# Keys and queries loaded as 32x32 blocks and transposed by VectorE in a fused linear-attention and MLP kernel

## The chip, the cores and the metric

The kernel runs on one core of one Trainium2 chip. The metric is device time in microseconds (us) from launch to end of one execution.

## What is computed

The reference is a complex-decay linear attention followed by a two-layer MLP, all in float32:

```
for t in range(S):                       # S = 768, state S_re/S_im is 48 x 48 per (batch, head)
    S_re, S_im = a_t * (S_re + i S_im)   # a_t complex, its magnitude cut at 0.999
    S_re += outer(k_t, v_t)
    y_t = q_t @ S_re
x = y reshaped to (B*S, H*D)             # 3072 x 384
h = x @ w_in;  g = gelu(h);  out = g @ w_out   # 384 -> 2048 -> 384
```

There are 4 batches and 8 heads, so 32 (batch, head) lanes, of head size 48.

## The kernel before

**Lanes.** The recurrence over `t` is turned into scaled keys and queries. The 768 steps are cut into four groups (`GROUPS`) of two chunks each: groups 0 and 1 with chunks of 64 steps, groups 2 and 3 with chunks of 128. Partitions hold (batch, head, chunk) twice, once for rows ahead of the middle of a chunk and once for rows behind it. Each group is worked through in slices of 8 rows (`tick`): `normalise` cuts the magnitude of `a`, `scan` multiplies the decays up row by row on VectorE (tiles `tt`, `bt`), and `towards` and `against` scale the keys and queries in tile `xt`. `against` then writes `xt` to a scratch buffer in DRAM, `kq{g}`, with three DMAs for each slice: one of 768-byte rows and two of 384-byte rows. `kq{g}` is laid out as (batch, head, chunk), step, (key, query), 96 numbers.

**Units.** A unit is 128 steps of one batch, all 8 heads; there are 24 (units 0 to 7 come from groups 0 and 1, units 8 to 15 from group 2, units 16 to 23 from group 3). `unit(u)` loads its keys and queries in one DMA into `kqn` (two such tiles take turns; 1024 rows of 768 bytes, a step to a partition) and its values into `vn`. The keys are used twice. With a step to a partition they are the weights with which `add_state` adds to the state `st`. For the scores they are needed with the 96 numbers on the partitions, so `turn` transposes keys and queries, 8 heads each, with 16 TensorE transposes against `ident_r` into the PSUM banks `att`, and copies these out to `kps` and `qTs` tiles on ScalarE or VectorE. `scores` multiplies, VectorE masks (`kp<-att,causal`), `y` collects the output in PSUM, and the unit ends with its rows split into a high and a low part in `xT` (ScalarE `hi`, VectorE `lo`).

**Blocks.** Two or three units make a block (`BLOCKS` = 2, 3, 3, 3, 3, 3, 3, 2, 2: units 8, 9, 10 are block 3, units 14, 15, 16 block 5). `block(j)` runs 16 steps: `first` (matmuls `ph<-xT,wi_hi` and `wi_lo`, gelu on ScalarE into `gh` and `gf`, the difference `gl` on VectorE) and `second` (matmuls `po<-wo_hi` and `wo_lo`). The first matmul of a block needs the `xT` of all of its units. The units of the next block are put between the steps of a block. At its end a block copies each `po` bank to an output tile and stores it. These output tiles (`ots`) are six halves of the three `raw` tiles, into which the weights were loaded at the start.

**Weights and checks.** At the start the weights are loaded into `raw` and split in two parts by VectorE, ScalarE and TensorE (`weights`, scratch tile `wh`). Later they are read a second time for a range check (`check_range`, DMAs `a<-in_moe_w_in_dram`).

**The order of the work.** All instructions are first collected as steps; `Plan.order` then simulates the engines with a table of costs (`FIXED`, `EACH`, `BYTES`, ...) and writes one fixed order for each engine. It takes the best of several passes, the first of which is ranked with the offsets `MORE`; `BIAS` steers steps that may go to either of two engines. All DMAs go through SyncE's queue (SP) in that order, and an instruction that waits holds up what stands behind it on its engine.

Of the kernel before, what the change touches and what calls it, by code (L numbers as in the profile page):

```python
# [10 lines left out]
F32 = mybir.dt.float32  # L11
# [9 lines left out]
B, H, S, D = 4, 8, 768, 48  # L21
D2 = 2 * D
BH = B * H
C = 128
# [4 lines left out]
GROUPS = ((0, 64), (128, 64), (256, 128), (512, 128))  # L29
NG = len(GROUPS)  # L30
NP = 2 * NG

UNITS = [[(b, t, C)] for t in range(0, S, C) for b in range(B)]
DM = H * D
# [23 lines left out]
def dap(t, offset, dims):  # L58
    return bass.AP(t.tensor, t.offset + offset, dims)


def vap(t, dims):
    t = t[:] if not isinstance(t, bass.AP) else t
    return bass.AP(t.tensor, t.offset, [list(t.ap[0])] + dims)
# [11 lines left out]
TABLE = 1.3  # L76
ISSUE = 0.9
FETCH = 2.2
BYTES = 3.6e5

ROUND, PASS = 0.462e-3, 0.4219e-3

# [9 lines left out]
EARLIER, N_RAW, N_KP = 1, 3, 2  # L92
PASSES = 4
N_A = 4
WL = 0.307

MORE = dict(lanes0=473.93, lanes1=-159.43, lanes2=-833.73, lanes3=415.48, weights0=-32.30, weights1=-241.94, units0=543.37, units1=1360.34, units2=638.43, blocks0=-158.78, blocks1=286.22, blocks2=576.59, checks=842.20)
BIAS = dict(vector=0.35, scalar=-0.41, gpsimd=6.75)


class Step:
# [8 lines left out]
class Plan:  # L110
# [54 lines left out]
    def add(self, calls):  # L165
        step = Step()
        n = len(self.steps)
        engine = calls[0][0]
        cost = 0.08 * (engine == "scalar" and len(calls) > 1)
        for call in calls:  # L170
            outs, ins = self.operands(call)
            cost += self.cost(call, outs, ins)
            if engine == "tensor":
                step.form = ("turn" if call[1] == "transpose" else "round" if call[3]["rhs"].dtype == F32R else
                             "slim" if call[3]["lhsT"].shape[1] <= 32 else "narrow" if call[3]["lhsT"].shape[1] <= 64 else "full")
            if engine == "sync":
                step.data = max(0.05, math.prod(c for _, c in outs[0].ap) * 4 / BYTES)
            for x in tuple(call[2]) + tuple(call[3].values()):
                step.table = TABLES.get(x, step.table) if isinstance(x, AF) else step.table
            for x, writes in [(x, False) for x in ins] + [(x, True) for x in outs]:  # L180
                self.hold(step, n, x, writes)
        step.options[engine] = calls, cost
        self.ports(step, engine, calls)
        if self.behind is not None:
            step.before.add(self.behind)
        step.before.discard(n)
        step.chain, step.weight = self.chain.get(engine, (None, 1.0))
        step.kind, step.part = self.kind, self.part
        self.steps.append(step)
# [71 lines left out]
    def natural(self):  # L261
# [4 lines left out]
        for i in range(len(steps) - 1, -1, -1):  # L266
# [9 lines left out]
            rest[i] = t  # L276
        return [t + MORE[s.kind] for t, s in zip(rest, steps)]

    def forward(self, rank):
# [14 lines left out]
        while len(order) < len(steps):  # L294
            best = None
            for e, waiting in pool.items():
# [8 lines left out]
                if len(steps[i].options) > 1:  # L305
                    ends = {o: max(free[o], ready[i], port[other[o]] if o in steps[i].port else 0.0) + c + BIAS[o] for o, (_, c) in steps[i].options.items()}
                    if ends[e] > min(ends.values()) + 1e-9:
# [106 lines left out]
def lanes_and_chunks(ctx, tc, flags, a_lanes, x_lanes, v_units, w_in, w_out, out):  # L414
    nc = tc.nc
    pool = lambda name, bufs, **kw: ctx.enter_context(tc.tile_pool(name=name, bufs=bufs, **kw))
    cst = pool("cst", 1)
    dram = pool("dram", 1, space=DRAM)
    ps = pool("ps", 1, space=PSUM)
    P = Plan(nc, loose=[flags])  # L420

    def ring(name, shape, n, dtype=F32, pool=cst):
        return itertools.cycle([pool.tile(shape, dtype, name=f"{name}{i}", tag=f"{name}{i}")[:] for i in range(n)])
# [41 lines left out]
    kq = [dram.tile([64, c, 2, D2], F32, name=f"kq{g}") for g, (_, c) in enumerate(GROUPS)]  # L465


    wide = w_in.dtype == U32
    own = [ps.tile([128, 512], F32, name=f"att{i}", tag=f"att{i}")[:] for i in range(3)]
    ph = [ps.tile([128, 512], F32, name=f"ph{i}", tag=f"ph{i}")[:] for i in range(2)]  # L470
# [1 line left out]
    for p in own:  # L472
        nc.vector.memset(p, 0.0)
    ps_h = itertools.cycle(ph)
    raws = ring("raw", [128, DM * (2 if wide else 1)], N_RAW, w_in.dtype)

    wh = cst.tile([128, DM], U32, name="wh")[:]

# [59 lines left out]
    def rows(s):  # L538
        g, i, r0, nt = slices[s]
        return g, i, r0, nt, nt + last_of(s)  # L540
# [4 lines left out]
    def load_a(s):  # L545
        g, i, r0, nt, nr = rows(s)
        a3 = next(a3s)
        at = 2 * D * (GROUPS[g][0] // 4 + g + r0)
        P.sync.dma_start(out=a3[:, 1:3, 0:nr, :], in_=a_lanes[:, at:at + 2 * D * nr].rearrange("p (c r d) -> p c r d", c=2, d=D))
        tiles[s] = {"a3": a3}  # L550

    def load_x(s):
        g, i, r0, nt, nr = rows(s)

        xs[s] = next(xts)[:, 0:nt]
        at = 2 * D * (GROUPS[g][0] // 4 + r0)
        P.sync.dma_start(out=xs[s][:, :, 1], in_=x_lanes[:, at:at + 2 * D * nt].rearrange("p (r c d) -> p r c d", c=2, d=D))
# [74 lines left out]
    def against(s):  # L632

        g, i, r0, nt, nr = rows(s)
        T = tiles[s]
        td, te, xt = T["td"], T["te"], xs[s]
        P.both("tensor_tensor", out=td, in0=T["b2"], in1=te, op=ALU.mult)
        P.vector.scalar_tensor_tensor(out=td, in0=td, scalar=2.0, in1=te, op0=ALU.subtract, op1=ALU.mult, reverse0=True)
        P.both("tensor_tensor", out=td, in0=td, in1=xt[:, :, 1, 1], op=ALU.mult)
        P.both("tensor_tensor", out=xt[:, :, 1], in0=vap(td, [[D, nt], [0, 2], [1, D]]), in1=T["bo"], op=ALU.mult)  # L640
        w, size = 2 * D2, GROUPS[g][1]
        P.sync.dma_start(out=dap(kq[g], (size // 2 - 1 - r0) * w, [[size * w, 64], [-w, nt], [1, w]]), in_=xt[0:64])
        for c in range(2):
            P.sync.dma_start(out=dap(kq[g], (size // 2 + r0) * w + c * D2, [[size * w, 64], [w, nt], [1, D2]]), in_=xt[64:128, :, 1 - c])
        if s + 2 < end:
            load_x(s + 2)
        if s + N_A < end:
            load_a(s + N_A)
# [39 lines left out]
    def tick(s):  # L688
# [20 lines left out]
        with P.work(part=f"b{s}"):  # L709
            if back is not None:  # L710
                towards(back)
                against(back)
        with P.work(part=f"s{s}"):
            scan(s)
        if last_of(s):
            with P.work(part=f"e{s}"):
                squares_b(s)
                ending(s)
                logs(s, None)
                towards(s)  # L720
                against(s)
# [48 lines left out]
    def unit(u):  # L770
# [3 lines left out]
        chunks, row = [], 0  # L774
        for b, t, n in UNITS[u]:
            for i in range(NP):
                g, m = divmod(i, 2)
                t0, size = GROUPS[g][0] + m * GROUPS[g][1] - t, GROUPS[g][1]
# [14 lines left out]
        kqn = next(kqns)  # L793
        kn, qn = kqn[:, :, 0], kqn[:, :, 1]
        vn = next(vns)
        w = 2 * D2
        _, g, m, _, size, b = chunks[0]
        P.sync.dma_start(out=kqn, in_=dap(kq[g], (b * H * 2 + m) * size * w, [[w, C], [2 * size * w, H], [1, w]]))
        P.sync.dma_start(out=vn, in_=v_units[u])

        held = []
# [54 lines left out]
        qT, kT = [], []  # L856

        def turn(src, dst, ring, halves=(0, 1)):
            some = [next(ps_att) for _ in halves]
            with P.together():  # L860
                for hh, p in zip(halves, some):
                    for j in range(4):
                        P.tensor.transpose(out=p[0:D2, j * 128:(j + 1) * 128].bitcast(F32R), in_=src[:, hh * 4 + j, :].bitcast(F32R), identity=ident_r[:])
            for p in some:
                t = next(ring)
                p = p[0:D2, :].rearrange("p (j l) -> p j l", j=4)
                P.either(("scalar", "copy", (t[0:D2], p), {}), ("vector", "tensor_copy", (t[0:D2], p), {}))
                dst.append(t)
# [39 lines left out]
        if early:  # L908
# [11 lines left out]
            for c in with_state:  # L920
                add_state(c, turned[c])
        else:
            turn(kn, kT, kps)
            turn(qn, qT, qTs)
            scores()
# [16 lines left out]
        j = next(j for j in range(len(BLOCKS)) if u < first_unit[j + 1])  # L942
        if u == first_unit[j]:
            xblk[j] = next(xTs)
        xt = xblk[j][:, u - first_unit[j]]
# [9 lines left out]
    ghs, gls = ring("gh", [128, BLK * C], EARLIER + 1, F32R), ring("gl", [128, BLK * C], EARLIER + 1, F32R)  # L955
    gfs = ring("gf", [128, BLK * C], 1)

    ots = itertools.cycle([r.bitcast(F32)[:, c:c + DM] for r in [next(raws) for _ in range(N_RAW)] for c in range(0, r.shape[1], DM)])

    def block(j, between):  # L960
        nt = BLOCKS[j]
# [45 lines left out]
    def ticks(g):  # L1007
        P.chain["vector"] = "lanes", WL
        with P.work(f"lanes{g}"):
            for s in range(end):  # L1010
                if slices[s][0] == g:
                    tick(s)
        P.chain.pop("vector")
# [8 lines left out]
    for u in range(BLOCKS[0]):  # L1022
        with P.work("units0", f"u{u}"):
            unit(u)
    for j, more in enumerate(BLOCKS[1:] + (0,)):
        at = {(2 * i + 1) * NFT // (2 * more): first_unit[j + 1] + i for i in range(more)}
# [154 lines left out]
def tile_complex_linear_attention_moe(ctx, tc, q, k, v, a_re, a_im, w_in, w_out, a_lanes, x_lanes, v_units, w_pieces, out):  # L1181
# [9 lines left out]
    with ExitStack() as fast:  # L1191
        fast.enter_context(tc.manual_schedule())
        lanes_and_chunks(fast, tc, flags, a_lanes, x_lanes, v_units, w_in, w_out, out)
# [81 lines left out]
```

## Time and profile before

| | us |
|---|---|
| median of 3 runs | 673.92 (672.75 to 674.58) |
| the profiled execution, its own time | 674.9 |
| span of the profiled execution | 673.1 |

The span runs from the first to the last instruction on record; the time of the execution is 1.8 us more. PE is TensorE's matmuls, PEld its weight loads, DVE is VectorE, ACT ScalarE, POOL GpSimd, SPq the queue of SyncE that issues DMAs. PEclk is the granted TensorE clock as a share of full speed. All instructions of the plan have line 403, that of the helper that issues them, so that groups are told apart by their tiles.

### The profile page before, as it was taken

To read this page: it belongs to the slowest core of one execution; us is meant where nothing else is said; L and a number is where in the kernel's file an instruction comes from. 1 tells how busy PE (TensorE), PEld (TensorE's weight loads), DVE (VectorE), ACT (ScalarE), POOL (GpSimd) and SP (SyncE) were. 2 spreads that over 40 slices of the span, in tenths; PEclk is the share of its full clock that TensorE was granted. 3 is DMA by queue.
4 is the path that set the end of the run, shared out by engine and by line. 5 is a ranking of instruction groups with operands and counts; after the bars stand their busy time and mean duration, and the time that the engine had idled before them with its cause. 6 is when DMAs were issued, how large, how long until landed. Compare 5 with 4: busy or idle time off the path is not lost.

```text
span 673.1 us, 16301 instructions
## 1 busy us (share of the span) xinstructions
PE 627.9 (93%) x6570; PEld 574.2 (85%) x6570; DVE 451.3 (67%) x1128; ACT 445.2 (66%) x1012; POOL 21.2 (3%) x65
## 2 busy tenths in 40 slices
PE   4566599998999999999999999999999999999995
PEld 2233378887889999999999999999999999999995
DVE  7999979998999999999999972442331221131221
ACT  7556658887888898978889775437634653556532
POOL 2001000030000000102000000000000000000000
PEclk9777789999999999999999999999999999999999
DMA  8388958586366657766777556442444161032000
GB/s 268 94 211 220 252 150 234 161 226 213 102 156 171 142 125 175 186 163 167 189 222 208 109 131 198 134 106 103 131 119 133 40 201 48 24 118 83 25 1 27
DMA packets 134354, 97.07 MB, mean 144 GB/s; under 512 B 69248, under 2 KB 126592, under 8 KB 134272
## 3 DMA queue, kind: packets, MB, share of 16 engines
q1 hardware_dynamic: 134272, 95.96, 52.5%
q8 instruction: 53, 0.87, 0.5%
q14 instruction: 29, 0.24, 0.1%
HBM read 69.40 MB, written 23.59 MB: 138 GB/s over the span
## 4 chain that ended last, share of the span: by engine, by line
PE 81%; DVE 9%; DMA 5%; ACT 2%; issue 1%; SPq 1%; DVEq 0%
PE po L403 32%; PE ph L403 30%; PE att L403 19%; DVE a L403 2%; DMA raw<-in_moe_w_in_dram 2%; DVE tt L403 1%; DMA kqn<-kq 1%; DVE xt L403 1%; DVE bt L403 1%; DMA raw<-in_moe_w_out_dram 1%; DVE wh L403 1%; SPq L403 1%; DMA kq<-xt 1%; DVE raw L403 1%; DVE tab L403 1%
## 5 line engine op out<-in xcount | busy, mean ns | idle before, releaser
L403 PE MATMUL ph<-xT,wi_hi 128*128 128x384 f32 (+1 forms) x864 | 207.3, 321 | 0.0
L403 DVE TENSOR_TENSOR gl<-gf,gh 128x384 fp32r<-128x384 f32 (+1 forms) x144 | 73.9, 513 | 150.6 <-ACT gf L403 145.2
L403 PEld LDWEIGHTS ph<-xT,wi_hi 128*128 128x128 f32 x864 | 153.8, 188 | 2.3 <-issue 0.4
L403 ACT ACTIVATE gh<-ph 128x384 fp32r<-128x384 f32 (+1 forms) x144 | 65.6, 456 | 126.6 <-PE ph L403 125.9
L403 PE MATMUL ph<-xT,wi_lo 128*128 128x384 f32 (+1 forms) x432 | 137.1, 317 | 0.0
L403 PE MATMUL po<-wo_hi,gh 128*128 128x384 f32 x384 | 132.9, 346 | 0.1
L403 PE MATMUL po<-wo_lo,gh 128*128 128x384 f32 x384 | 128.7, 335 | 0.0
L403 PE MATMUL po<-wo_hi,gl 128*128 128x384 f32 x384 | 92.5, 342 | 0.6 <-DVE gl L403 0.6
L403 PEld LDWEIGHTS ph<-xT,wi_lo 128*128 128x128 f32 x432 | 81.2, 188 | 0.0
L403 PEld LDWEIGHTS po<-wo_hi,gh 128*128 128x128 f32 x384 | 72.2, 188 | 2.5 <-ACT gh L403 0.9
L403 PEld LDWEIGHTS po<-wo_lo,gh 128*128 128x128 f32 x384 | 72.3, 188 | 0.1
L403 ACT ACTIVATE gf<-ph 128x384 f32<-128x384 f32 (+1 forms) x144 | 65.1, 452 | 4.9 <-DVE gl L403 3.4
L403 DVE TENSOR_TENSOR tt<-bt,a 128x192 f32<-128x192 f32 x192 | 67.0, 349 | 0.2
L403 PEld LDWEIGHTS po<-wo_hi,gl 128*128 128x128 f32 x384 | 65.1, 188 | 2.0 <-DVE gl L403 1.1
L403 DVE TENSOR_TENSOR bt<-tt 128x96 f32<-128x96 f32 x192 | 47.9, 249 | 0.2
L403 PEld LDWEIGHTS att<-qT,kp 96*64 96x64 f32 (+1 forms) x512 | 39.8, 170 | 2.3 <-issue 1.3
L403 PE MATMUL att<-qT,kp 96*64 96x64 f32 (+1 forms) x512 | 41.7, 256 | 0.0
L403 ACT ACTIVATE a<-a 128x384 f32<-128x384 f32 (+1 forms) x72 | 38.6, 539 | 3.9 <-DMA a<-in_moe_w_in_dram 2.4
L403 DVE TENSOR_TENSOR kp<-att,causal 128x512 f32<-128x512 f32 x48 | 31.8, 683 | 12.9 <-PE att L403 11.1
L403 PE MATMUL po<-raw,ident_r 128*128 128x384 f32 x64 | 31.3, 573 | 8.5 <-issue 2.6
L403 PEld LDWEIGHTS att<-ident_r,kqn 128*96 128x96 f32 x384 | 32.8, 127 | 5.6 <-ACT kp L403 1.3
L403 PE MATMUL att<-ident_r,kqn 128*96 128x128 f32 x384 | 35.7, 236 | 1.9 <-ACT kp L403 1.1
(153 smaller groups left out, 929.7 us busy)
## 6 DMA issues: line engine op xcount, KB each, us to landing
kqn<-kq SPq DMA_DIRECT2D x24, 768.0 KB, 6.3
xt<-in_x_lanes_dram SPq DMA_DIRECT2D x24, 384.0 KB, 4.0
kq<-xt SPq DMA_DIRECT2D x24, 384.0 KB, 4.1
kq<-xt SPq DMA_DIRECT2D x48, 192.0 KB, 4.5
a<-in_a_lanes_dram SPq DMA_DIRECT2D x20, 384.0 KB, 3.4
raw<-in_moe_w_in_dram SPq DMA_DIRECT2D x16, 384.0 KB, 5.2
raw<-in_moe_w_out_dram SPq DMA_DIRECT2D x16, 384.0 KB, 5.0
vn<-in_v_units_dram SPq DMA_DIRECT2D x24, 256.0 KB, 5.6
```

The lines of the kernel that those rows point to most:

```text
L403: getattr(getattr(self.nc, engine), name)(*args, **kw)
```

## The change

- For units 8 to 23 (`u >= UDT`) the one load into `kqn` is replaced by six loads into a tile `blk`, for keys and queries and for each third of the 96 numbers. Each load fills 32 partitions with 1024 runs of 128 bytes: 32 steps on the partitions, and for each head and each 32 steps a run of 32 numbers, so that `blk` holds 32x32 blocks in their places but each not yet transposed. There is one `blk`, and it lies in the memory of the three `raw` tiles.
- `turn` for these units is two VectorE transposes (each 96 partitions x 4 heads x 128, block by block) straight into the `kps` or `qTs` tile: four for a unit. The 16 TensorE transposes and the four copies from PSUM are gone.
- The keys with a step to a partition are still loaded for units 8 to 19, whose state is still added to: 1024 rows of 384 bytes.
- The scratch of groups 2 and 3 (`apart`) has the chunk as its outermost dimension, so that a head and its 32-step blocks lie at one stride. Each slice of these groups is written in six DMAs of 32 lanes rather than three of 64.
- The output tiles are two tiles of their own, `wh` and a new `ot`, in place of six halves of `raw`.
- The planner's cost of a DMA counts packets (`PACKET`, `BYTES`), and its offsets `MORE` and `BIAS` have other values, so that the order of all engines may differ.

```diff
-BYTES = 3.6e5
+PACKET, BYTES = 0.5e-3, 2.96e-6
...
+UDT = 8
-MORE = dict(lanes0=473.93, lanes1=-159.43, lanes2=-833.73, lanes3=415.48, ...
-BIAS = dict(vector=0.35, scalar=-0.41, gpsimd=6.75)
+MORE = dict(lanes0=575.74, lanes1=-377.35, lanes2=-812.79, lanes3=221.09, ...
+BIAS = dict(vector=0.07, scalar=-0.61, gpsimd=7.10)
...
-                step.data = max(0.05, math.prod(c for _, c in outs[0].ap) * 4 / BYTES)
+                some = math.prod(c for _, c in outs[0].ap)
+                step.data = max(0.05, some / min(run(x) for x in outs + ins) * PACKET + some * 4 * BYTES)
...
+    apart = [GROUPS[g][1] == C and any(u >= UDT and ... ) for g in range(NG)]
...
-    raws = ring("raw", [128, DM * (2 if wide else 1)], N_RAW, w_in.dtype)
+    raw_all = cst.tile([128, N_RAW, max(DM * (2 if wide else 1), -(-16 * C // N_RAW))], w_in.dtype, name="raw_all")[:]
+    raws = itertools.cycle([raw_all[:, i, 0:DM * (2 if wide else 1)] for i in range(N_RAW)])
...
-        P.sync.dma_start(out=dap(kq[g], (size // 2 - 1 - r0) * w, [[size * w, 64], [-w, nt], [1, w]]), in_=xt[0:64])
-        for c in range(2):
-            P.sync.dma_start(out=dap(kq[g], (size // 2 + r0) * w + c * D2, [[size * w, 64], [w, nt], [1, D2]]), in_=xt[64:128, :, 1 - c])
+        n = 2 if apart[g] else 1
+        for m in range(n):
+            at = m * BH * size * w
+            P.sync.dma_start(out=dap(kq[g], at + (size // 2 - 1 - r0) * w, [[size * w, 64 // n], [-w, nt], [1, w]]), in_=xt[m:64:n])
+            for c in range(2):
+                P.sync.dma_start(out=dap(kq[g], at + (size // 2 + r0) * w + c * D2, [[size * w, 64 // n], [w, nt], [1, D2]]), in_=xt[64 + m:128:n, :, 1 - c])
...
-        P.sync.dma_start(out=kqn, in_=dap(kq[g], (b * H * 2 + m) * size * w, [[w, C], [2 * size * w, H], [1, w]]))
+        if u < UDT:
+            P.sync.dma_start(out=kqn, in_=dap(kq[g], base, [[w, C], [lane, H], [1, w]]))
+        else:
+            for c in range(2):
+                for j in range(D2 // 32):
+                    P.sync.dma_start(out=blk[j * 32:(j + 1) * 32, c].rearrange("p h (i d) -> p (h i) d", d=32),
+                                     in_=dap(kq[g], base + c * D2 + j * 32, [[w, 32], [32 * w, H * C // 32], [1, 32]]))
+            if chunks[-1][0] < NP - 1:
+                P.sync.dma_start(out=kn, in_=dap(kq[g], base, [[w, C], [lane, H], [1, D2]]))
...
         def turn(src, dst, ring, halves=(0, 1)):
+            if u >= UDT:
+                c = 0 if src is kn else 1
+                for hh in halves:
+                    t = next(ring)
+                    P.vector.transpose(out=t[0:D2], in_=blk[0:D2, c, hh * 4:hh * 4 + 4])
+                    dst.append(t)
+                return
...
-    ots = itertools.cycle([r.bitcast(F32)[:, c:c + DM] for r in [next(raws) for _ in range(N_RAW)] for c in range(0, r.shape[1], DM)])
+    ots = itertools.cycle([wh.bitcast(F32), cst.tile([128, DM], F32, name="ot")[:]])
+    blk = raw_all.rearrange("p i n -> p (i n)").bitcast(F32)[:, 0:16 * C].rearrange("p (c h l) -> p c h l", c=2, h=H)
```

## Rows read from the trace of the kernel before

**Rows 1.** The page: busy time by engine, and its 40 slices.
```profile
PE 627.9 (93%) x6570; PEld 574.2 (85%) x6570; DVE 451.3 (67%) x1128; ACT 445.2 (66%) x1012; POOL 21.2 (3%) x65
...
PE   4566599998999999999999999999999999999995
```

**Rows 2.** The page: the chain that ended last, by engine.
```profile
PE 81%; DVE 9%; DMA 5%; ACT 2%; issue 1%; SPq 1%; DVEq 0%
```

**Rows 3.** Windows by stage: length, busy us (x instructions), PEclk, DMA share, GB/s.
```profile
core 0: us, PE busy (x) PEld busy (x) DVE busy (x) ACT busy (x) POOL busy (x), PEclk, DMA share, GB/s
0.00:160.00 160.00, 122.68 (x1195) 86.83 (x1196) 145.25 (x385) 109.99 (x232) 12.81 (x43) 0.87 0.74 208
...
278.00:327.00 49.00, 48.65 (x622) 47.17 (x621) 48.13 (x123) 39.15 (x90) 4.72 (x9) 1.00 0.70 173
278.00:400.00 122.00, 121.65 (x1484) 118.39 (x1483) 117.78 (x299) 101.42 (x214) 4.72 (x9) 1.00 0.67 171
400.00:535.00 135.00, 135.00 (x1401) 132.38 (x1400) 43.67 (x81) 67.77 (x184) 2.50 (x10) 1.00 0.43 121
```

**Rows 4.** Timeline of PE around unit 8's key transposes: start, us, instruction.
```profile
286.55 0.69 PE L403 MATMUL att<-ident_r,kqn 128*96 128x128 f32 x8
287.08 0.58 PE L403 MATMUL ph<-xT,wi_hi 128*128 128x384 f32 x2
...
288.02 0.51 PE L403 MATMUL ph<-xT,wi_hi 128*128 128x384 f32 x2
```

**Rows 5.** Groups on PE from 278 to 600 us: busy, mean ns, idle.
```profile
L403 PE MATMUL att<-ident_r,kqn 128*96 128x128 f32 x256 | 22.5, 230 | 0.3 <-DVE kp L403 0.3
```

**Rows 6.** Copies from PSUM from 280 us: ns min/median/max, first and last start.
```profile
L403 ACT COPY kp<-att x28: 563/584/617, 299.4 to 585.8; 96x512 f32<-96x512 f32 x28
L403 ACT COPY qT<-att x32: 563/586/645, 289.6 to 593.2; 96x512 f32<-96x512 f32 x32
L403 DVE COPY kp<-att x4: 675/680/682, 287.5 to 325.8; 96x512 f32<-96x512 f32 x4
```

**Rows 7.** Timeline of SP, the stretch in which group 2 ends.
```profile
275.13 2.93 SPq L403 DMA_DIRECT2D kq<-xt  x3
280.86 1.00 SPq L403 DMA_DIRECT2D kqn<-kq  x2
```

**Rows 8.** Windows that hold one load of xt, two of m, one write of kq.
```profile
373.00:375.00 2.00, 2.00 (x18) 2.00 (x17) 2.00 (x8) 1.97 (x4) 0.00 (x0) 1.00 0.82 200
437.50:441.50 4.00, 4.00 (x33) 3.95 (x32) 1.77 (x5) 3.59 (x9) 0.00 (x0) 1.00 0.23 37
229.50:231.50 2.00, 2.00 (x37) 1.93 (x34) 2.00 (x7) 1.76 (x4) 0.00 (x0) 1.00 0.94 173
```

**Rows 9.** DMA issues: count, KB each, median us from issue to landing.
```profile
kqn<-kq SPq DMA_DIRECT2D x24, 768.0 KB, 6.3
out_dram<-raw SPq DMA_DIRECT2D x24, 192.0 KB, 2.1
```

**Rows 10.** Timelines: unit 10's last transposes (PE), its xT (DVE), block 3's first matmul (PE).
```profile
314.22 0.69 PE L403 MATMUL att<-ident_r,kqn 128*96 128x128 f32 x8
...
323.21 0.54 DVE L403 TENSOR_TENSOR xT<-att,xT 128x384 fp32r<-128x384 f32 x1
...
326.82 0.41 PE L403 MATMUL ph<-xT,wi_hi 128*128 128x384 f32 x1
```

**Rows 11.** Timelines at the end of block 4: copies, stores, then the next block's matmuls.
```profile
468.95 0.89 ACT L403 COPY raw<-po 128x384 f32<-128x384 f32 x2
469.21 1.31 SPq L403 DMA_DIRECT2D out_dram<-raw  x3
...
472.75 0.42 PE L403 MATMUL po<-wo_hi,gh 128*128 128x384 f32 x1
```

**Rows 12.** Timeline of SP, the stretch in which group 3 ends.
```profile
398.95 2.92 SPq L403 DMA_DIRECT2D kq<-xt  x3
...
405.81 2.82 SPq L403 DMA_DIRECT2D kqn<-kq  x2
```

More of the change, by code (lines that the diff above doesn't have):

```diff
@@ L95, with run @@
 WL = 0.307
-MORE = dict(lanes0=473.93, lanes1=-159.43, lanes2=-833.73, lanes3=415.48, weights0=-32.30, weights1=-241.94, units0=543.37, units1=1360.34, units2=638.43, blocks0=-158.78, blocks1=286.22, blocks2=576.59, checks=842.20)
-BIAS = dict(vector=0.35, scalar=-0.41, gpsimd=6.75)
+UDT = 8
+MORE = dict(lanes0=575.74, lanes1=-377.35, lanes2=-812.79, lanes3=221.09, weights0=-149.78, weights1=-103.19, units0=636.83, units1=1302.69, units2=549.34, blocks0=-201.58, blocks1=340.05, blocks2=534.64, checks=865.08)
+BIAS = dict(vector=0.07, scalar=-0.61, gpsimd=7.10)
+def run(x):
+    n = 1
+    for step, count in reversed(x.ap):
+        if step != n:
+            break
+        n *= count
+    return n
 class Step:
@@ L465, in lanes_and_chunks @@
     kq = [dram.tile([64, c, 2, D2], F32, name=f"kq{g}") for g, (_, c) in enumerate(GROUPS)]
+    apart = [GROUPS[g][1] == C and any(u >= UDT and GROUPS[g][0] <= t < GROUPS[g][0] + 2 * C for u, some in enumerate(UNITS) for _, t, _ in some) for g in range(NG)]
     wide = w_in.dtype == U32
@@ L797, in unit @@
         _, g, m, _, size, b = chunks[0]
-        P.sync.dma_start(out=kqn, in_=dap(kq[g], (b * H * 2 + m) * size * w, [[w, C], [2 * size * w, H], [1, w]]))
+        base, lane = ((m * BH + b * H) * size * w, size * w) if apart[g] else (b * H * 2 * size * w, 2 * size * w)
+        if u < UDT:
[7 more added lines that the diff above has]
+                P.sync.dma_start(out=kn, in_=dap(kq[g], base, [[w, C], [lane, H], [1, D2]]))
         P.sync.dma_start(out=vn, in_=v_units[u])
```

## The prediction, made before the change was timed

> **What bounds the kernel now.** I read the page first: TensorE's matmuls are busy for 627.9 us of 673.1, and the row of slices shows where the rest is, nearly all in the first quarter; after that it is 9s to the end [rows 1]. The chain that ended last says the same from the other side: 81% of it are TensorE's own instructions, one after the other [rows 2]. Then the windows by stage, for what lies beside TensorE: from 278 to 400 us, while group 3's lanes run, TensorE is busy 121.65 us of 122 and VectorE 117.78 of 122; from 400 to 535 us VectorE has only 43.67 us of work in 135 [rows 3]. So from 278 us on a microsecond taken off TensorE is a microsecond of the span, as long as what TensorE is to work on arrives in time. What must arrive is told by unit 10: it is the last of block 3, and block 3's first matmul comes at 326.82, just 3 us after the unit's `xT` is done at 323.75 (323.21 + 0.54) [rows 10]. The change alters how units 8, 9 and 10 get there, so this is the place to watch. Before it, units 0 to 7 and all of groups 0 and 1 keep their work.
>
> **What is taken off TensorE.** Unit 8's eight key transposes start at 286.55 and the next matmul at 287.08: 0.53 us, and the pair behind them takes 0.58 where a pair in the run of the same work takes 0.51 [rows 4]. That is 0.60 us for eight, 1.20 us for the 16 of a unit, and 19.2 us for 16 units. (The busy time of the 256, 22.5 us [rows 5], counts overlapping instructions, so it is an upper bound; 256 at 0.53 for eight, 17.0 us, is the lower.) TensorE's clock is full in all these stretches (1.00, that is 2.4 GHz [rows 3]), so no other price applies.
>
> **What VectorE and ScalarE get.** ScalarE loses 60 copies of 0.58 us [rows 6], off the path. VectorE gets four transposes of 96x512 for a unit; no such instruction is in the trace. The nearest row is VectorE's copy of the same shape, 0.68 us [rows 6]. As a lower bound I take half of that, as an upper one twice: 0.34 to 1.36. I take 0.68, being one element per lane and step as in the copy: 2.7 us for a unit. The Trainium skill (VectorE: DVE Perf Modes, The three transpose paths) gives 311 ns for a 128x128 transpose in a two-byte type; four times the elements would make an estimate of 1.24 us by that page, near my upper bound, and no run here shows it. Units 8 to 15 fall into VectorE's full stretch: 8 x 2.7 less the four copies that VectorE made itself (2.7) is 19 us more for group 3's lanes, which end with the writes at 398.95 to 401.9 [rows 12]. I cost that at nothing: the first unit that needs group 3 is unit 16, a unit of block 5, and block 4 ends only at about 469 [rows 11]. With 19 us more, unit 16's load is issued at 425 rather than 405.8 [rows 12] and the unit is ready by about 450, before 469 less the gain. Without that cover each microsecond past it would cost one.
>
> **What the loads cost.** Six loads of 1024 runs of 128 bytes are 6144 packets for a unit, against 1024 of 768 bytes; the keys' own load (1024 of 384 bytes) comes on top up to unit 19. Three windows price packets. One load of `xt`, 1024 packets of 384 bytes, is a DMA share of 0.82 over 2 us: 0.82 x 2 x 16 / 1024 = 25.6 ns each. Two swaps of `m`, 768 packets of 192 bytes, are 0.23 over 4 us: 19.2 ns [rows 8]. So half the bytes cost three quarters: the line through both gives 17.1 ns at 128 bytes, 6.6 us for a unit over 16 engines. Upper bound: a 128-byte packet costs no more than one of 384, 9.8 us; lower: in proportion to its bytes (8.5 ns), 3.3 us. The third window, 64 partitions written to `kq` at 173 GB/s [rows 8], says that few partitions may be slow; at that rate the 786 KB would take 4.5 us, inside the bounds.
>
> The two `m` rows also weigh a rule. The Trainium skill (DMA: Bandwidth & Descriptors, Why small descriptors are slow) counts 32-byte beats and three more cycles for a packet: at the DMA's 850 MHz an estimate of 10.6 ns for 192 bytes and 8.2 ns for 128. The window shows 19.2 ns for 192, nearly twice, so the row decides; by the page a unit's load would be 3.2 us, no link would be late, and the time would be that of the second case below.
>
> **The link to block 3.** `blk` is one tile, where `kqn` are two: a unit's loads wait until the unit before has transposed. Before, both loads could go out at 280.86 and unit 8's transposes began at 286.55 [rows 4, 7]. Now unit 8's six go out at 281 (its chunk's writes are issued ahead of the other chunk's, so the three added writes cost nothing; if the load waits for all six, 2 us). First issue 0.4, packets 6.6, landing as for a small store 2.1 [rows 9]: 9.1 us (5.8 to 12.3). Four transposes at 2.7: 11.8 us for a unit (7.2 to 17.7 with both upper prices), so unit 10 is transposed at 281 + 35 = 316 (303 to 334). From its last TensorE transposes, done at 314.75 (314.22 + 0.53), to `xT` at 323.75 the trace takes 9 us [rows 10]: `xT` at 325 (312 to 343). TensorE without three units' transposes would come to block 3 at 326.8 - 3.6 = 323. The stall is 2 us with the queue empty. It isn't: DMA's share from 278 to 327 is already 0.70 of 49 us, 34 us [rows 3], and 20 us of 128-byte packets come in. One microsecond of queueing for each unit makes it 5 us; I take 5 (0 to 20). Later links have room: blocks 3 and 4 run from 326.82 to about 469 [rows 10, 11], some 71 us each for three units, over 20 us a unit, and after 400 us the DMA share is 0.43 [rows 3].
>
> **Smaller parts.** Two output tiles: the third copy of a block waits for the first store, issued at 469.21, to land 2.1 us later [rows 9, 11], and then copies for 0.45: ready at 471.8. The next block first writes the third bank at 472.75 [rows 11], so it lies hidden by 1 us; at other block ends it may miss, and I take 1 us in all (0 to 6). Added kq writes: 48 issues of some 1 us (2.93 for three [rows 7]) on SP, spread over groups 2 and 3, behind which stand the lanes' own loads, issued ahead of need: nothing (2 us if the last slice of group 2 is on the path). Other planner offsets: every engine's order can change, above all in the first 160 us, where TensorE is idle 37 us [rows 3]; 0, with 4 either way.
>
> **Sum.** 19.2 off, 5 and 1 back: 13.2 us. From the profiled execution, span 673.1 and 1.8 around it, that is 661.7; the median of the runs lies 1.0 below the profiled execution, so 660.7, and I forecast 661.
>
> **Rivals.** *Full gain.* If packets cost near the lower bound, or units 8 to 10 are loaded while something else fills TensorE, no link is late: 673.9 - 19.2 = 655, a little less with a better start. For it: 11 us of slack in the lower case (312 against 323). Against: the 19.2 ns row. *The loads take the gain.* If a unit takes 17.5 us from load to load (9.8 us of packets, transposes at 1.36, a queue in between), unit 10 has its `xT` at 281 + 52 + 9 = 342, block 3 starts 19 us late, and the time is within 0.3% of before: 672 to 676. *Slower.* TensorE's order is fixed: where it was written for data that come earlier than they do, the unit's score matmuls wait and everything queued behind them on TensorE with them. If each load is 2 us later than the order assumes and units follow each other without spare time, 16 units lose 32 us, 13 more than the gain: 687. It decides from 1.2 us for a unit. For it: units run one after the other from 286 us on with VectorE at 97% and DMA at 0.67 [rows 3]; against: after 400 us there is air in both, and a delayed unit leaves blocks to work on. That the change does nothing can be left out, since the transposes are gone from TensorE's stream for certain.
>
> **Numbers.** The forecast (part of the gain, 656 to 672) 0.50; full gain or better (under 656) 0.22; within 0.3% (2 us, about what a measurement of this kernel can tell from no change) 0.10; slower 0.18. Faster is the first two, 0.72. The range 651 to 678 leaves out a better start on top of the full gain and the larger half of the slower case; the forecast's own range is 656 to 672.
>
> **What would show it.** In the profile after: 256 transposes fewer on PE and no `att<-ident_r` from 278 us on; VectorE transposes of about 0.68 us; `blk` loads of 6.6 us of DMA for a unit; PE idle, if at all, between 315 and 345 us, released by VectorE's transposes (`kp`, `qT`) or, at block 3, by `xT`; group 3's last write near 420 us; out copies without waits. Wrong would make it: PE waiting on transposes at most units (the slower rival), transposes above 1.4 us, packets above 26 ns, or a first quarter that moves by more than 4 us.

## The result, and the profile after

The changed kernel takes 667.98 us (median of 4 runs, 664.51 to 668.87) against 674.25 (672.75 to 675.35) of the kernel before beside it: a ratio of 0.990 [0.986, 0.994], or 6.8 us less, where 13 were forecast. The profiled execution has a span of 666.8 us and a time of 668.8. One execution of the run `old_offsets` took 1196.91 us, in a slow state; it is left out below, and with it that kernel's only trace.

The page after: busy time by engine, the slices of PE, and the chain that ended last by engine.

```profile
PE 614.3 (92%) x6314; PEld 559.2 (84%) x6314; DVE 482.2 (72%) x1179; ACT 425.9 (64%) x989; POOL 19.6 (3%) x65
...
PE   5374799999999999999899999998999999999995
...
PE 63%; DVE 17%; ACT 7%; DMA 7%; issue 3%; SPq 1%; POOL 0%; DVEq 0%; ACTq 0%
```

TensorE has 256 matmuls fewer than in [rows 1]. But an 8 stands among the 9s in slices 20 and 28 (from 316.7 and from 450.1 us, 16.67 us each), and the chain that was TensorE's for 81% [rows 2] is now TensorE's for 63%: VectorE and DMAs have come into it. The windows by stage say where:

```profile
0.00:160.00 160.00, 124.33 (x1195) 89.07 (x1195) 146.89 (x393) 111.23 (x233) 10.58 (x37) 0.85 0.73 210
...
278.00:400.00 122.00, 114.86 (x1252) 109.64 (x1252) 112.47 (x271) 87.27 (x198) 1.75 (x5) 0.99 0.96 177
...
278.00:460.00 182.00, 172.79 (x1883) 165.68 (x1883) 150.07 (x353) 121.64 (x281) 2.98 (x10) 0.99 0.91 173
```

From 278 to 400 us TensorE was busy all but 0.35 us [rows 3]; now 7.14 us are missing. The DMA share, 0.67 there [rows 3], is 0.96. For the last stretch the kernel before has:

```profile
278.00:460.00 182.00, 181.65 (x2154) 177.25 (x2153) 140.54 (x342) 131.71 (x298) 7.21 (x19) 1.00 0.62 162
```

Idle time of TensorE from 278 to 460 us is 0.35 us before and 9.21 after. Its waits after, from 258 to 470 us (us in total, times, longest):

```profile
PE att L415 <- DVE kp L415: 3.9, 3, 2.5
PE att L415 <- DVE st L415: 1.7, 1, 1.7
PE att L415 <- DVE qT L415: 1.6, 1, 1.6
PE po L415 <- ACT gh L415: 1.4, 4, 0.6
PE ph L415 <- ACT gh L415: 1.0, 3, 0.5
PE po L415 <- ACT ot L415: 0.3, 1, 0.3
```

All but 0.2 us of the first three are four places in the timeline of PE: the scores of units 9, 11 and 13, and a product of unit 16 with the state.

```profile
303.72 2.05 PE L415 MATMUL att<-qT,kp 96*128 96x128 f32 x16 [1.18 <-DVE kp L415]
...
328.30 2.24 PE L415 MATMUL att<-qT,kp 96*128 96x128 f32 x16 [2.50 <-DVE kp L415]
...
363.91 2.19 PE L415 MATMUL att<-qT,kp 96*128 96x128 f32 x16 [1.61 <-DVE qT L415]
...
454.51 1.08 PE L415 MATMUL att<-qT,st 96*32 96x128 f32 x32 [1.73 <-DVE st L415]
```

Why the transposes come late is seen on VectorE: it stands for 2.68 us ahead of unit 11's, for a DMA into `blk` (`raw_all` in the views). Some 5 us ahead of unit 13's it has stood for 2.72 us for the state's swap `m<-st`, a DMA, and is busy from there on. Up to 452.85 it stands 3.05 us for another of these swaps.

```profile
302.95 1.30 DVE L415 STREAM_TRANSPOSE kp<-raw_all 96x512 f32<-96x512 f32 x2 [1.39 <-DMA raw_all<-kq]
...
312.96 1.26 DVE L415 STREAM_TRANSPOSE kp<-raw_all 96x512 f32<-96x512 f32 x2
...
321.36 0.54 DVE L415 TENSOR_TENSOR xT<-att,xT 128x384 fp32r<-128x384 f32 x1
...
324.58 1.30 DVE L415 STREAM_TRANSPOSE qT<-raw_all 96x512 f32<-96x512 f32 x2 [2.68 <-DMA raw_all<-kq]
...
356.23 0.56 DVE L415 TENSOR_TENSOR m<-m,gg 96x384 f32<-96x384 f32 x1 [2.72 <-DMA m<-st]
...
452.85 0.56 DVE L415 TENSOR_TENSOR st<-st,gg 96x384 f32<-96x384 f32 x1 [3.05 <-DMA m<-st]
```

The timeline of SP shows the loads of units 8 to 11. Successive ones are 9.2 to 13.8 us apart, since each needs room in the one `blk` and its turn in the queue: unit 11's goes out 3.0 us after the last transposes of unit 10 (312.96 + 1.26), behind a swap and two other loads.

```profile
281.20 4.67 SPq L415 DMA_DIRECT2D raw_all<-kq  x6
...
290.39 7.89 SPq L415 DMA_DIRECT2D raw_all<-kq  x6
...
303.45 5.87 SPq L415 DMA_DIRECT2D raw_all<-kq  x6
...
314.48 1.30 SPq L415 DMA_DIRECT2D m<-st  x2
...
317.26 6.88 SPq L415 DMA_DIRECT2D raw_all<-kq  x6
...
351.07 1.57 SPq L415 DMA_DIRECT2D m<-st  x2
...
438.74 7.65 SPq L415 DMA_DIRECT2D raw_all<-kq  x6
...
447.36 1.30 SPq L415 DMA_DIRECT2D m<-st  x2
```

The last two lines are the state's wait: the swap stands behind the six block loads of unit 17, is issued at 447.36 and ends VectorE's wait at 452.85, 5.5 us later. The swap at 351.07, behind five of unit 13's loads, ends the wait at 356.23. The instructions on the tile itself (ns min/median/max, first and last start):

```profile
L415 SPq DMA_DIRECT2D raw_all<-kq x96: 325/793/3552, 281.2 to 572.0; - x96
L415 DVE STREAM_TRANSPOSE qT<-raw_all x32: 664/667/709, 288.2 to 591.5; 96x512 f32<-96x512 f32 x32
L415 DVE STREAM_TRANSPOSE kp<-raw_all x32: 662/697/708, 290.0 to 590.4; 96x512 f32<-96x512 f32 x32
```

What a unit's load costs the DMA engines is read where almost nothing else runs, from 496 to 499 us:

```profile
496.00:499.00 3.00, 3.00 (x19) 3.00 (x18) 1.37 (x3) 0.94 (x3) 0.00 (x0) 1.00 1.02 154
```

The DMA share is 1.02, so the engines are full, at 154 GB/s. The 786 KB of a unit take 5.1 us at that rate, and a packet 5.1 x 16 / 6144 = 13.3 ns.

**An account.** For a profile let idle be span less PE's busy time, clock loss be (1 - mean granted clock) x span, and work be busy time less clock loss: an estimate of what TensorE had to do at full clock. Before: 673.1 - 627.9 = 45.2 idle, 0.032 x 673.1 = 21.5 clock, 606.4 work. After: 52.5, 26.7, 587.6. So work fell by 18.8 us, idle rose by 7.3 and clock loss by 5.2. These three numbers are what the experiments are to explain. How good the account is, the runs below tell: kernels with the very same 6314 matmuls come out between 582.8 us of work (`price_only`) and 588.4 (`double_turn`), so that a difference of two works is good to some 3 us, more or less.

### The profile page after: what moved, and what is told of

It is laid out like the page before. It is cut to its first block, busy times and chain, and to the rows that moved or that the text cites. A ratio compares the mean times of both kernels' runs of the same rounds, so it can differ in the third digit from the quotient of the medians.

```text
span 666.8 us, 16041 instructions
## 1 busy us (share of the span) xinstructions
PE 614.3 (92%) x6314; PEld 559.2 (84%) x6314; DVE 482.2 (72%) x1179; ACT 425.9 (64%) x989; POOL 19.6 (3%) x65
## 4 chain that ended last, share of the span: by engine, by line
PE 63%; DVE 17%; ACT 7%; DMA 7%; issue 3%; SPq 1%; POOL 0%; DVEq 0%; ACTq 0%
PE po L415 26%; PE ph L415 24%; PE att L415 13%; DVE a L415 4%; DVE tt L415 3%; DVE bt L415 2%; DMA raw_all<-kq 2%; DVE xt L415 2%; ACT a L415 2%; SPq L415 1%; DVE gl L415 1%; DVE kp L415 1%; ACT tab L415 1%; DVE tab L415 1%; DMA a<-in_moe_w_out_dram 1%
## 5 line engine op out<-in xcount | busy, mean ns | idle before, releaser
L415 PE MATMUL po<-wo_hi,gl 128*128 128x384 f32 x384 | 91.1, 338 | 0.0
L415 ACT ACTIVATE a<-a 128x384 f32<-128x384 f32 (+1 forms) x77 | 41.4, 539 | 21.1 <-DMA a<-in_moe_w_in_dram 7.5
L415 PE MATMUL po<-raw_all,ident_r 128*128 128x384 f32 x64 | 32.1, 586 | 10.8 <-DVE raw_all L415 7.1
L415 ACT ACTIVATE a<-a,by_partition 128x384 f32<-128x384 f32 x53 | 33.8, 637 | 1.2
L415 ACT ACTIVATE a<-tab 128x384 f32<-128x384 f32 (+1 forms) x45 | 23.9, 534 | 9.8 <-DVE tab L415 9.7
```

Of the source, the lines that this page charges most:

```text
L415: getattr(getattr(self.nc, engine), name)(*args, **kw)
```

## The experiments

The theory: the transposes are worth some 19 us, and the loads of `blk` arrive later than the order, written by a planner that costs them too low, assumes; TensorE then waits in the middle of a fixed order. The rivals: the loss comes from the other offsets (another order from the start), or from VectorE, or the transposes were worth less.

**The change without the new transposes** (`no_turn`). No unit is loaded as blocks, so the scratch keeps its old layout and its three writes for a slice, too. The offsets, the planner's costs and the two output tiles of the diff stay. Units 12 to 15 and 20 to 23, of a group's second chunk, read the first chunk's rows, the same amount of them.

```diff
-UDT = 8
+UDT = 24
```

> The changed kernel with the limit of units set to 24, so that no unit is loaded as blocks or transposed by VectorE and the scratch keeps its layout; the planner's new offsets and packet costs and the two output tiles stay. If the gain comes from the transposes taken off TensorE (my theory), this is the kernel before within 0.5%: 671 to 677 us. If the new order or the output tiles carry the gain (rival), it is near the changed kernel, 666 to 670. If they cost what is missing of the gain (second rival), it is slower than before by 4 us and more: 678 to 684.

688.6 us (684.3 to 690.3), ratio 1.019 [1.014, 1.023]: the theory's 671 to 677 was missed, and the second rival is nearest. That is 12.6 us over before by the ratio, with the side changes alone, and more than they were priced at by any theory. Much of it lies at the start: a granted clock of 0.82 in the first 160 us, against 0.87 [rows 3], and 3.6 us of idle time from 160 to 278. What offsets set for another program can cost is shown by the run after the next.

**Half of the units** (`udt16`). Only group 3's units take the new way. Units 12 to 15 read the first chunk's rows.

```diff
-UDT = 8
+UDT = 16
```

> Only units 16 to 23 are changed, those after the lanes, where VectorE and the DMA queues have room. Theory (each unit is worth 1.2 us and the missing part is lost in waits of TensorE for units 9 to 14): 8 units give 9.6 us with next to no wait, 663 to 666 us, and TensorE's idle time from 278 to 460 us is under 2 us. Rival (a unit is worth less than counted, 6.3 us over 16, 0.4 each): 3 us, 670 to 672.

678.56 us (671.9 to 681.75), ratio 1.006 [1.002, 1.009]. The theory's 663 to 666 was missed, and so was the rival's 670 to 672. TensorE's idle time from 278 to 460 us is 1.4 us, under 2 as the theory said; the loss lies at the start, with a clock of 0.83 in the first 160 us and 3.9 us of idle time from 160 to 278. A version with offsets of its own stands last.

**The changed kernel with the offsets of before** (`old_offsets`).

```diff
-MORE = dict(lanes0=575.74, ...
-BIAS = dict(vector=0.07, ...
+MORE = dict(lanes0=473.93, ...
+BIAS = dict(vector=0.35, ...
```

> The changed kernel with the planner's offsets MORE and BIAS as they were before. Theory (offsets move the order of the work, not its amount): within 4 us of the changed kernel, 664 to 672, with waits of TensorE between 278 and 460 us at other units. Rival (the new offsets are what makes the loads fit): slower than before, 676 and more.

687.2 us (686.0 to 689.2), ratio 1.020 [1.016, 1.023]. The theory's 664 to 672 was missed and the rival held: offsets belong to their program, and a wrong set costs some 20 us here, more than all that is looked for. From here on causes are told apart in kernels that keep one order.

**The same order, other packets** (`wide_packets`). The order is written as in the changed kernel; when a block load is issued, it reads 32 runs of 4096 bytes in place of 1024 of 128. Bytes and partitions are the same, the numbers loaded are other ones.

```diff
+if engine == "sync" and "raw_all" in kw["out"].tensor.name and "kq" in kw["in_"].tensor.name:
+    o, i = kw["out"], kw["in_"]
+    kw = dict(out=bass.AP(o.tensor, o.offset, [list(o.ap[0]), [1, 8 * C]]),
+              in_=bass.AP(i.tensor, i.offset, [[8 * C, 32], [1, 8 * C]]))
```

> The changed kernel in the same order, but each block load takes the same 131 KB as 32 runs of 4096 bytes rather than 1024 of 128, so that the numbers that come are other ones. Theory (TensorE waits for the loads of the next unit): the waits of TensorE at units 9, 11 and 14 (1.2, 2.5, 1.6 us) and the clock's fall behind the second (1.7) go, 660 to 663 us. Rival (what is missing lies in the order and in VectorE, not in the loads): no change, 666 to 669.

658.63 us (657.6 to 659.35), ratio 0.977 [0.974, 0.980]: 8.8 us under the changed kernel (0.0131 of before), and a little under the 660 to 663 expected. Its window from 278 to 460 us, its waits of PE from 258 to 470 us and the tile's loads:

```profile
278.00:460.00 182.00, 180.72 (x2052) 175.37 (x2051) 155.91 (x367) 126.26 (x297) 2.97 (x10) 1.00 0.80 185
```

```profile
PE po L418 <- ACT gh L418: 1.1, 2, 0.6
PE ph L418 <- ACT gh L418: 0.5, 1, 0.5
```

```profile
L418 SPq DMA_DIRECT2D raw_all<-kq x96: 302/419/1333, 282.0 to 560.0; - x96
```

The waits for `kp`, `qT` and `st` are all gone, and idle time in the stretch falls from 9.21 to 1.28 us. VectorE's work and the order are unchanged. So what comes late are the loads, and the swaps behind them, through the packets; the transposes alone, as many as VectorE has here, make TensorE wait for none of them. Whether the packets hold up the DMA engines more or the issuing queue was not separated: both get lighter (a DMA share of 0.80 for 0.91, 419 ns for 793). The expectation calls the third unit that TensorE waited for unit 14; it is unit 13.

**The transposes put back in the same order** (`pe_back`). Ahead of each changed unit's scores TensorE does 16 transposes of a constant, whose results are overwritten.

```diff
... (ahead of a unit's first att<-qT,kp)
+for _, _, _, kw in s.calls * 2:
+    self.nc.tensor.transpose(out=kw["out"][0:D2].bitcast(F32R), in_=self.ident_r[:, 0:D2], identity=self.ident_r[:])
```

> The changed kernel in the same order, with 16 TensorE transposes of a constant put in front of each changed unit's score matmuls, into the bank that these overwrite: TensorE's old work on top of the new way. Theory (a unit's transposes are worth 1.2 us of TensorE, and TensorE sets the time): 16 x 1.2 = 19 us slower than the changed kernel, less what falls into its present waits of some 7 us: 680 to 687. Rival (a unit is worth less than counted, 0.4 us): 674 to 676.

678.01 us (672.6 to 680.8), ratio 1.005 [1.0005, 1.009]: 10.1 us above the changed kernel, under the 12 at which the expected range begins, and over the rival's 674 to 676. Unit 8's transposes, and the group of all 256:

```profile
291.76 1.25 PE L418 MATMUL att<-ident_r 128*96 128x128 f32 x16
```

```profile
L418 PE MATMUL att<-ident_r 128*96 128x128 f32 x256 | 20.2, 232 | 0.9 <-DVE xT L420 0.9
```

The work comes back (603.0 us by the account, 15.4 more), but 4.9 us of idle go, since the transposes fill time in which TensorE had waited. What the change takes off TensorE is partly time that it then waits.

**VectorE's transposes twice** (`double_turn`).

```diff
+if engine == "vector" and name == "transpose":
+    self.nc.vector.transpose(*args, **kw)
```

> The changed kernel in the same order, with each VectorE transpose issued twice, 64 more of 0.67 us, 43 us of VectorE. Theory (TensorE waits mainly for the loads; VectorE's transposes stand in the same link): the units from 8 to 15 pass 1.3 to 2.7 us later each while VectorE is full, some of it into waits of TensorE: 670 to 678. Rival (VectorE is the limit of the stretch from 278 to 420 us and each of its microseconds counts there): 22 us, 688 to 692. Second rival (VectorE's work is hidden): no change, 666 to 669.

683.17 us (678.8 to 685.2), ratio 1.011 [1.008, 1.015]: 14.5 us more for 64 x 0.667 = 43 us of VectorE, between theory and rival. The waits for `kp` from 258 to 470 us:

```profile
PE att L417 <- DVE kp L417: 10.3, 10, 2.3
```

Of each added microsecond of VectorE about a third reaches the time: VectorE is not the bound, but it is a part of the same link.

**Block loads at dearer prices** (`priced`). The planner charges a packet 0.65 ns in place of 0.5, and SP 0.74 us in place of 0.45 for a load of 32 partitions. The offsets are chosen for this table. The expectation says that the trace shows both of these prices. It does for the issue, 0.793 us in the median, but not for the packet: by the planner's formula a block load takes 1024 x 0.5 ns = 0.51 us for its packets and 131072 x 2.96e-6 = 0.39 for its bytes, 0.90 us in all, and 1.05 with the new price, where the window above gives 5.1 / 6 = 0.85. So the packet was dear enough before, and is now priced above what was read.

```diff
-PACKET, BYTES = 0.5e-3, 2.96e-6
+PACKET, BYTES = 0.65e-3, 2.96e-6
...
-return FIXED[engine] * (1 if 32 < outs[0].shape[0] < 128 else 0.73)
+return FIXED[engine] * (1.2 if outs[0].shape[0] == 32 else 1 if 32 < outs[0].shape[0] < 128 else 0.73)
...
+MORE = {'lanes0': 568.37, 'lanes1': -369.31, 'lanes2': -813.55, 'lanes3': 215.84, 'weights0': -90.32, ...
+BIAS = {'vector': 0.42, 'scalar': -0.8, 'gpsimd': 7.1}
```

> The changed kernel with the block loads at the price that its trace shows in the planner's table (0.65 ns in place of 0.5 for a packet, an issue of 0.74 us in place of 0.45 for 32 partitions) and with offsets chosen for this table. Theory (TensorE waits because its order was written for loads that come earlier): TensorE's waits for VectorE's transposes and masks between 278 and 460 us, 7.2 us now, fall under 3 us, and the time is that of the changed kernel or up to 4 us less, 662 to 669, since a right price shortens no load. Rival (the waits come from something else): waits as before, or a time above 672.

653.34 us (652.98 to 659.66), ratio 0.973 [0.967, 0.978]: it beats both kernels, and by more than expected. Windows, then the waits of PE from 258 to 460 us:

```profile
0.00:160.00 160.00, 124.29 (x1243) 89.96 (x1245) 152.92 (x412) 118.21 (x252) 10.67 (x43) 0.89 0.75 213
160.00:278.00 118.00, 114.29 (x1441) 105.80 (x1437) 115.64 (x300) 102.68 (x205) 3.64 (x7) 1.00 0.63 148
278.00:460.00 182.00, 181.21 (x2160) 176.47 (x2158) 151.55 (x343) 126.94 (x324) 4.59 (x15) 1.00 0.93 183
```

```profile
PE po L415 <- ACT gh L415: 1.5, 3, 1.0
PE ph L415 <- ACT gf L415: 0.8, 1, 0.8
PE po L415 <- ACT ot L415: 0.3, 1, 0.3
```

With loads of 128-byte packets TensorE no longer waits for a transpose. Of the 15.4 us of span under the changed kernel, 4.9 are idle time and 8.5 clock, of which (0.89 - 0.85) x 160 = 6.4 lie in the first 160 us. The latter has nothing to do with the units. Of the idle time, 8.4 us are won from 278 to 460 us (0.79 against 9.21) and 3.1 are lost from 160 to 278 (busy 114.29, after the change 117.39). So prices and offsets were run apart.

**The new prices with the changed kernel's offsets** (`price_only`), and **the new offsets with its prices** (`offsets_only`). Each has one half of the diff above.

> The changed kernel with the truer prices for block loads in the planner's table, and its own offsets. It tells whether the right price alone did what the version with right price and offsets chosen for it showed (653). Theory (a right price takes the waits at units 9 to 14 away; offsets that were not chosen for the table cost elsewhere): TensorE waits under 3 us for VectorE's transposes and masks between 278 and 460 us, and a time between 660 and 675, with the loss in other places. Rival (the offsets alone gave the gain): waits as in the changed kernel, 668 and more.

666.64 us (665.2 to 670.7), ratio 0.989 [0.986, 0.992]. Its wait of PE for transposes from 258 to 460 us, and two windows:

```profile
PE att L415 <- DVE kp L415: 0.5, 2, 0.3
```

```profile
0.00:160.00 160.00, 120.38 (x1203) 86.05 (x1204) 150.97 (x401) 114.01 (x239) 12.97 (x43) 0.86 0.74 213
...
278.00:460.00 182.00, 177.91 (x1928) 172.78 (x1928) 153.03 (x355) 123.02 (x291) 4.84 (x13) 0.99 0.95 178
```

> The changed kernel with its own price table and the offsets that were chosen for the truer prices. Theory: the order is again written for loads that come earlier than they do, so TensorE waits 4 us and more for VectorE's transposes and masks from 278 us on, 664 to 680. Rival (the offsets alone gave the gain): 652 to 657.

671.99 us (669.8 to 674.45), ratio 0.997 [0.994, 1.000]. Its two largest waits of PE in the same stretch, and the window:

```profile
PE po L415 <- ACT gh L415: 7.6, 7, 1.9
PE att L415 <- DVE kp L415: 2.7, 5, 1.4
```

```profile
278.00:460.00 182.00, 172.60 (x1883) 165.72 (x1883) 149.46 (x346) 124.77 (x302) 2.96 (x10) 0.99 0.95 177
```

The prices alone take the waits for transposes from 5.5 us to 0.5, but give the time back in the first 160 us, where PE is busy 4 us less. The offsets alone leave waits of 2.7 us (4 and more were expected) and add some for ScalarE. TensorE's idle time from 278 to 460 us shows both halves side by side: 9.21 us in the changed kernel, 9.40 with the new offsets alone, 4.09 with the new prices alone (1.7 for an `xT` and 1.7 for a gelu are the largest waits), 0.79 with both. So the dearer loads in the table take the waits for transposes away, and the offsets alone don't; but neither half explains 653, and each of these four is a single order.

**The transposes put back in the priced order** (`priced_pe_back`). The edit is that of `pe_back`.

> The version with truer prices (653), in its own order, with 16 TensorE transposes of a constant put in front of each changed unit's score matmuls. There TensorE hardly waits, so by the theory nothing of them can hide: 16 x 1.16 = 18.5 us more, 670 to 673, against 10 in the order of the changed kernel. Rival (the order, not the waits, decides what they cost): 10 us again, 663.

671.25 us (670.8 to 677.7), ratio 0.998 [0.995, 1.001]. Its window:

```profile
278.00:460.00 182.00, 181.50 (x2155) 177.04 (x2154) 148.52 (x334) 121.46 (x308) 3.59 (x10) 1.00 0.87 171
```

It lies in the range expected, 17.9 us above `priced` by the medians, 17.3 by the ratios; by the account work rises by 18.6 us, while idle time stays at 47.6 and clock loss at 17 to 18. Here nearly all of the transposes' work is time. By the intervals the 17.3 us and the 10.1 of `pe_back` are each good to some 4 us, so that 18.6 lies within reach of the first and not of the second.

**Half of the units, with offsets of their own** (`udt16_tuned`). Units 12 to 15 read their own chunk.

```diff
-UDT = 8
+UDT = 16
...
-b * H * 2 * size * w
+(b * H * 2 + m) * size * w
... (MORE and BIAS with values chosen for this program)
```

> Units 16 to 23 alone changed, as in the run of that split, but with offsets chosen for this split (and with the load of an unsplit scratch of 128-step chunks at its own chunk). Theory (the offsets, not the units, cost the first try its time): 4 us or more under that run's 678.6, 667 to 674, with next to no waits of TensorE for transposes. Rival (units 16 to 23 are worth nothing): 676 to 680.

664.7 us (663.9 to 665.45), ratio 0.987 [0.984, 0.989]: 9.1 us under before, and a little better than the 667 to 674 expected. Work is 596.1 us, 10.3 less than before, where half of 18.8 is 9.4. So half of the transposes, in units whose loads had room, bring at least as much as all 16 did in the changed kernel. How much of that is a better start was not separated: block 1's first store comes at 254.7 us, at 261.3 before.

## Why the prediction was right, and which term failed

| us, profiled execution | span | idle | clock loss | work |
|---|---|---|---|---|
| before | 673.1 | 45.2 | 21.5 | 606.4 |
| after | 666.8 | 52.5 | 26.7 | 587.6 |
| `wide_packets` | 655.5 | 44.5 | 25.6 | 585.4 |
| `pe_back` | 677.0 | 47.6 | 26.4 | 603.0 |
| `priced` | 651.4 | 47.6 | 18.2 | 585.6 |
| `priced_pe_back` | 669.2 | 47.6 | 17.4 | 604.2 |

The forecast case, a part of the gain, 656 to 672, is the one that came, but with half of the gain forecast: 668 us where the sum gave 661. Step by step:

- **Taken off TensorE, 19.2 us.** Right: 18.8 by the account, and 18.6 between the two priced kernels (15.4 between `pe_back` and the changed kernel; the account is good to some 3).
- **VectorE's transposes, 0.68 us.** Right: 0.667 in the median for queries, 0.697 for keys. The Trainium skill (VectorE: DVE Perf Modes, The three transpose paths), from which 1.24 us was estimated, gives a price for two-byte numbers alone; the measurement decides.
- **The packets, 17.1 ns, 6.6 us for a unit.** Too high: 13.3 ns and 5.1 us, inside the bounds. The estimate by the Trainium skill (DMA: Bandwidth & Descriptors, Why small descriptors are slow (HBM only)) was 8.2 ns, so the row was nearer than the rule. The swaps of `m`, by which the rule was weighed, run between tiles, outside what that section's heading names; the block loads come from DRAM and are the fairer trial.
- **The link, 11.8 us for a unit and one of queueing.** Near, but by luck: the load of unit 12 begins at 329.03 and that of unit 8 at 281.20, 12.0 us for each of four units. The packets take 1.5 us less than forecast, and the queue takes more: SP needs 793 ns in the median for one of these loads, where 400 were taken for the first and nothing for the other five. The rest of the link was not taken apart. Unit 10 was transposed at 314.2 (forecast 316), and its `xT` was done at 321.9 (forecast 325).
- **The stall, 5 us at block 3.** This is the step that failed, in place and in size. Block 3 did not wait at all: its first matmul comes at 321.99, right behind unit 10's `xT` and with TensorE busy up to it.

```profile
321.99 0.51 PE L415 MATMUL ph<-xT,wi_hi 128*128 128x384 f32 x2
```

  TensorE waited for the units themselves: 1.18, 2.50 and 1.61 us ahead of scores, 1.73 for the state's swap, 2.4 for gelus (of which `wide_packets` still has 1.6). Those add up to 9.4 of the 9.9 us of waits, and of the four long ones only the second falls between 315 and 345 us, where idle time was forecast; 9.21 us are idle between 278 and 460, 8.9 more than before. The clock adds to it. After the 2.5 us stop the granted clock is this, from 328 to 334 us:

```profile
328.00:330.00 2.00, 1.70 (x15) 1.70 (x16) 2.00 (x6) 0.49 (x1) 0.00 (x0) 1.00 1.05 294
330.00:332.00 2.00, 2.00 (x10) 2.00 (x9) 2.00 (x4) 0.84 (x1) 0.00 (x0) 0.51 1.21 240
332.00:334.00 2.00, 2.00 (x9) 1.87 (x7) 2.00 (x6) 0.00 (x0) 0.00 (x0) 0.64 0.55 81
```

  First half speed, 1.2 GHz, then a mean between both levels: it costs 0.49 x 2 + 0.36 x 2 = 1.7 us. Together 10.6 us, where the stall and the output tiles were put at 6. The mechanism is that of the slower rival, a fixed order written for data that come earlier than they do; it had its place right, but not its size: 5.3 us ahead of scores where 32 were priced, since 3 units of 16 stopped TensorE for longer than 1 us, not all. `wide_packets` shows that the loads are the cause: with the same order and fewer packets these waits are gone. `price_only` shows that the planner's prices have a part in it: with dearer loads in the table 0.5 us of waits for transposes is left. What the planner had too low was the issue (0.45 us against 0.79), not the packet.
- **Output tiles, 1 us.** 0.3 us of waits on `ot`.
- **Group 3's lanes, hidden.** The last `kq` write goes out at 427.5, where 401 + 19 = 420 was forecast; its first unit is in block 5, and no wait for its data is among those above. The swap that TensorE waited 1.73 us for does stand behind the loads of its second unit.
- **Other offsets, 0 with 4 either way.** In the first 160 us 1.65 us less idle (124.33 against 122.68 busy [rows 3]), and 0.02 x 160 = 3.2 us more lost to the clock: some 1.6 us worse, inside the bound.

So 18.8 less 10.6 less 1.6 is 6.6, against 6.3 between the spans and 6.8 between the runs. That the sum closes proves little, since the account is made so that its parts add up to the span. Left open: how much of `priced` is its prices and how much a lucky order, since offsets and prices only worked together, and no second set of offsets was chosen for the old prices; which of the two prices did it, the issue's, which was too low, or the packet's, which went above what was read; and what two `blk` tiles would do, or block loads from a queue of their own, which were not tried.

## What to carry to other kernels

Work taken off the engine that bounds pays in full only if what replaces it arrives when the fixed order wants it: 18.6 us of transposes were worth 17 to 18 us in an order in which TensorE hardly waited, written with dearer loads, and 10 in one with 9 us of waits. So when a change adds a kind of transfer that the planner has not seen (few partitions, short runs), read its issue time and its packet price from the first trace, put them into the table, and choose the offsets anew before the order is judged. Here it was the issue time that was off. And test causes in a held order: with offsets set for another program the changed kernel came out 20 us worse, and the one with half of the units 14 us.

## What the runs showed of the hardware

- The time that a load takes to issue in SyncE's queue was longer with more packets: 793 ns in the median for 1024 packets of 128 bytes, 419 ns for 32 packets of 4096 (`wide_packets`), both into 32 partitions and both of 128 KB.
- Short packets do not cost in proportion to their bytes: 13.3 ns for 128 bytes, against 25.6 for 384 in a window of before [rows 8], half the time for a third of the bytes. At a DMA share of 1.02 the 128-byte loads moved 154 GB/s; a load of 384-byte packets moved 200 at a share of 0.82 [rows 8].
- A VectorE transpose of a 96x512 float32 tile in 32x32 blocks took 0.667 us in the median for queries and 0.697 for keys, about as long as VectorE's copy of the same shape from PSUM, 0.680 [rows 6].
- A stop of 2.5 us, after a stretch at a clock of 1.00, was followed by two windows of 2 us in which the granted clock was 0.51 and 0.64. After the stops of 1.18, 1.61 and 1.73 us it stayed at 1.00.
